# Rewriting the highway sum of a fused attention + highway kernel so that every VectorE step of it has an operand in PSUM

## The chip, the cores and the metric

One core of one Trainium2 chip. The metric is the device time of one execution in microseconds (us), medians over executions. An execution counts as slow when it lies more than 1.5% above the fastest of the same kernel; all runs told here are fast unless said. Engine names as in the profile: PE is TensorE, DVE VectorE, ACT ScalarE, POOL GpSimd, SP SyncE.

## The reference, cut to what matters

Cosine attention (8 batches, 12 heads, 448 positions, head size 64), then a highway layer over the 3584 x 768 result:

```python
def _moe_ref(x, w_h, w_t, b_t):
    H = np.maximum(x @ w_h, 0.0)
    T = 1.0 / (1.0 + np.exp(-(x @ w_t + b_t)))
    return (T * H + (1.0 - T) * x).astype(np.float32)
```

The kernel computes the sigmoid by tanh. With x standing for half of the reference's x, h for x @ w_h and t for tanh(x @ w_t + b_t/2), the result is (1+t) relu(h) - (t-1) x.

## The kernel before

The highway layer works in 28 tiles of 128 rows, each in two halves of 384 columns. Per half: 6 matmuls for the gate (plus one for the bias, or a bias add on DVE in the tail), 6 for h, tanh on ACT, and on DVE the gate g, the product and the output.

```python
def fg(ms=ms, mh=mh):                       # g = (t-1) x : two inputs in SBUF
    nc.vector.scalar_tensor_tensor(out=loc["g", mh][:, :], in0=loc["tt", mh][:, :],
        scalar=1.0, in1=xf()[:, ms], op0=ALU.subtract, op1=ALU.mult)
def fh(qi=qi, mh=mh):                       # h = (t+1) h : h in PSUM
    h = loc["pt", qi]
    nc.vector.scalar_tensor_tensor(out=h, in0=loc["tt", mh][:, :], scalar=1.0, in1=h, ...)
def fo(qi=qi, ms=ms, mh=mh):                # o = relu(h) - g
    nc.vector.scalar_tensor_tensor(out=loc["o"][:, ms], in0=loc["pt", qi], scalar=0.0,
        in1=loc["g", mh][:, :], op0=ALU.max, op1=ALU.subtract)
```

In the last six tiles (22 to 27; "the tail" below) both sums of a half lie in one two-bank PSUM tile, borrowed from the attention scores:

```python
if tail and w_i == 1 and grp[0] == 0:       # w_i == 1: the gate's matmuls, which come first
    loc["sp", mh] = s_ps.tile([128, 2, 512], FP32, name="sp")
...
loc["sp", mh][:, 1 - w_i, 0:MH] if tail else p_ps.tile([128, MH], FP32, name="pt", tag="pt")
```

The order of instructions on each engine comes from a list scheduler in the kernel (`Plan`), which models durations, buffers and the port that DVE and GpSimd share (`kind="lock"`). Semaphores are then set automatically, by tile. Strings such as `SQ_E` or `VM` assign each square, cast and copy to an engine.

## Time and profile before

| | kernel before |
|---|---|
| time, median | 292.5 us at the start, 291.5 to 291.9 in the later calls |
| granted PE clock in the profiled run | 0.98 |
| first output step of the highway layer | 59.1 us from the span's start |
| last output step before the tail (starts) | 246.6 us |
| last output step of all (starts) | 286.0 us |

The two positions in the middle of the table cut the run into a middle and a tail of 39.3 us; both kernels will be compared by them. One more view of the kernel before, ACT's timeline in the tail (start, duration, engine, line, operation, output and input, count; in brackets the idle time before it and what ended it):

```profile
265.83 0.49 ACT L847 ACTIVATE tt<-sp 128x384 f16<-128x384 f32 x1 [6.15 <-PE sp L818]
268.63 0.49 ACT L847 ACTIVATE tt<-sp 128x384 f16<-128x384 f32 x1 [2.32 <-PE sp L818]
```

Tanh reads the gate's sum, which was complete when the bias add ended, 0.8 us before each of the two tanhs; tanh was released by h's last three matmuls, which write the other bank of the same tile. That is how a wait by the whole tile looks: a releaser that computes nothing the waiter reads.

### The profile page before, as it was taken

Reading aid. Unit: us, or ns where it says so; the run is one execution under the profiler, and the core shown is the slowest. Engines: PE = TensorE matmul, PEld = TensorE weight load, DVE = VectorE, ACT = ScalarE, POOL = GpSimd, SP = SyncE. Lnnn points to the kernel's source line nnn. Section 1 sums busy time; section 2 is a strip of 40 time slices with the busy share of each in tenths; the row PEclk is TensorE's granted clock in tenths of the full one; section 3 lists DMA queues with packets and bytes.
Section 4 is the critical chain, followed back from the end, with each engine's and each line's share of the span. In section 5 each row is a group of like instructions: output and inputs, shape, how many; then the busy total and the mean of one; then the engine's idle time right before and its main releaser. Section 6 shows DMA issues by size and latency. Waiting matters only on the chain.

```text
span 290.9 us, 9872 instructions
## 1 busy us (share of the span) xinstructions
PE 244.1 (84%) x4229; PEld 137.8 (47%) x4229; DVE 238.2 (82%) x498; ACT 208.2 (72%) x284; POOL 138.6 (48%) x144
## 2 busy tenths in 40 slices
PE   0269777799888899999999999799999999887880
PEld 0226444454544455555545545356555555554440
DVE  3878918789999998999999989999975666696873
ACT  1398969979988899977987889668877767311120
POOL 3969558874468655962296836735900000000000
PEclk9999979989999999999999999999999999999996
DMA  7999929999999999999959999796757232112122
GB/s 259 375 353 292 257 52 309 212 284 326 247 273 243 287 179 369 289 182 284 356 123 248 164 287 283 146 235 132 157 119 147 85 85 56 56 56 81 56 108 54
DMA packets 72060, 58.94 MB, mean 203 GB/s; under 512 B 48336, under 2 KB 68304, under 8 KB 72016
## 3 DMA queue, kind: packets, MB, share of 16 engines
q1 hardware_dynamic: 70144, 55.49, 74.8%
q0 software_dynamic: 1600, 2.36, 4.5%
q8 instruction: 33, 0.54, 0.8%
q10 hardware_dynamic: 272, 0.46, 0.4%
q14 instruction: 11, 0.09, 0.1%
HBM read 38.14 MB, written 11.01 MB: 169 GB/s over the span
## 4 chain that ended last, share of the span: by engine, by line
PE 42%; DVE 25%; ACT 9%; DMA 7%; POOL 7%; issue 6%; SPq 2%; DVEq 0%; ACTq 0%; POOLq 0%
PE pt L818 17%; PE u L672 10%; PE sp L621 7%; ACT e L632 6%; DMA raw<-in_k_dram 6%; PE sp L818 5%; DVE g L851 3%; POOL qn L525 3%; DVE o L875 3%; DVE n L389 3%; DVE qn L525 3%; DVE x L723 2%; DVE pt L868 2%; DVE sp L837 2%; ACT tt L847 2%
## 5 line engine op out<-in xcount | busy, mean ns | idle before, releaser
L632 ACT ACTIVATE e<-sp 128x896 f16<-128x896 f32 x168 | 144.7, 920 | 21.3 <-PE sp L621 19.8
L818 PE MATMUL pt<-w,xT 128*128 128x384 f16 x528 | 102.3, 329 | 6.5 <-DVE o L875 3.4
L525 POOL TENSOR_TENSOR qn<-raw,rs 128x448 f16<-128x448 f32 x80 | 81.7, 1051 | 43.5 <-DVE rs L491 19.9
L818 PEld LDWEIGHTS <-xT 128*128 128x128 f16 x672 | 59.1, 98 | 62.5 <-issue 20.9
L621 PE MATMUL sp<-qT,qT 64*64 64x448 f16 x672 | 55.9, 379 | 8.3 <-ACT e L632 5.1
L672 PE MATMUL u<-vm,e 64*128 64x65 f16 x2688 | 58.3, 194 | 4.5 <-DVE x L723 3.4
L672 PEld LDWEIGHTS <-e 64*128 64x128 f16 x2688 | 48.7, 96 | 27.6 <-issue 17.2
L389 DVE TENSOR_REDUCE n<-sq 128x7 f32<-128x448 f16 x68 | 39.8, 609 | 2.9 <-ACT sq L365 2.4
L851 DVE SCALAR_TENSOR_TENSOR g<-tt,x 128x384 f16<-128x384 f16 x48 | 34.0, 708 | 9.3 <-ACT tt L847 9.2
L868 DVE SCALAR_TENSOR_TENSOR pt<-tt,pt 128x384 f32<-128x384 f16 x44 | 24.5, 557 | 9.1 <-PE pt L818 5.7
L847 ACT ACTIVATE tt<-pt 128x384 f16<-128x384 f32 x44 | 21.6, 492 | 14.2 <-ACT e L632 7.5
L621 PEld LDWEIGHTS <-qT 64*64 64x64 f16 x672 | 15.2, 106 | 33.5 <-issue 28.2
L818 PE MATMUL sp<-w,xT 128*128 128x384 f16 x144 | 25.4, 326 | 6.3 <-DVE o L875 2.9
L365 ACT ACTIVATE sq<-raw 128x896 f16<-128x896 f32 x29 | 26.9, 958 | 1.1 <-DMA raw<-in_k_dram 1.1
L847 ACT ACTIVATE tt<-sp 128x384 f16<-128x384 f32 x12 | 5.9, 490 | 29.9 <-DVE sp L837 16.9
L875 DVE SCALAR_TENSOR_TENSOR o<-pt,g 128x384 f32<-128x384 f32 x44 | 24.4, 554 | 1.3
L723 DVE TENSOR_TENSOR x<-u,rd 128x384 f16<-128x384 f32 x48 | 24.7, 552 | 0.7
L369 POOL TENSOR_TENSOR sq<-raw 128x448 f16<-128x448 f32 x17 | 17.7, 1038 | 15.0 <-DMA raw<-in_k_dram 6.1
L416 POOL TENSOR_TENSOR fold<-sq 128x448 f32<-128x448 f16 x14 | 15.0, 1085 | 13.4 <-ACT sq L365 13.4
L373 POOL TENSOR_TENSOR sq<-raw 128x448 f16<-128x448 f32 x17 | 17.8, 1049 | 0.0
L705 DVE RECIPROCAL rd<-u 128x12 f32<-128x12 f32 (+1 forms) x48 | 9.7, 202 | 9.9 <-PE u L672 9.4
L549 PE MATMUL tp<-ident,qn 128*128 128x128 f16 x63 | 6.7, 271 | 11.8 <-DVE qn L525 11.8
(46 smaller groups left out, 165.4 us busy)
## 6 DMA issues: line engine op xcount, KB each, us to landing
raw<-in_q_dram SPq DMA_DIRECT2D x24, 448.0 KB, 5.9
vr<-in_v_dram SPq DMA_DIRECT2D x24, 448.0 KB, 6.3
raw<-in_k_dram SPq DMA_DIRECT2D x23, 448.0 KB, 6.3
out_dram<-o SPq DMA_DIRECT2D x24, 384.0 KB, 3.9
out_dram<-o SPq DMA_DIRECT2D x8, 192.0 KB, 2.8
w<-in_moe_w_t_dram POOLq DMA_DIRECT2D x2, 576.0 KB, 10.2
w<-in_moe_w_h_dram POOLq DMA_DIRECT2D x2, 576.0 KB, 12.5
qT<-qn SPq DMA_TRANSPOSE x39, 4.5
```

The source lines that it names most:

```text
L365: nc.scalar.activation(o, i, AF.Square)
L389: nc.vector.reduce_sum(n2[:, qd, NT * t + g0 : NT * t + g0 + n], src()[:, g0 : g0 + n, 0:width], axis=AX.X,)
L525: (nc.vector if eng == "DVE" else nc.gpsimd).tensor_mul(st["qn", Q, t][:, :, :].rearrange("p c (h d) -> p h c d", h=2)[:, h0:h1, c0:c1, :] ...
L621: nc.tensor.matmul(sp[64 * half : 64 * half + 64, h, 0:S].rearrange("x (c p) -> x c p", c=C), lhsT=kT[hp, ci, 64 * half : 64 * half + 64], ...
L632: nc.scalar.activation(e[:, o : o + 2 * S].rearrange("x (a p c) -> x a p c", a=2, c=C), st["sp", Q, ci][:, :, 0:S].rearrange("x a (c p) -> ...
L672: nc.tensor.matmul(u[:, s, slot * (D + 1) : (slot + 1) * (D + 1)], lhsT=e[sp, o : o + 128], rhs=vm[sp, 2 * qd + h, c, 0 : D + 1], start=(c ...
L723: nc.vector.tensor_mul(st["x", b][:, :, 4 * qd : 4 * qd + 4, :].rearrange("p t (h s) d -> p t h s d", s=2)[:, :, :, s, :], u[:, s, :, 0:D] ...
L818: nc.tensor.matmul(loc["pt", qi], lhsT=loc["xT"][:, cc, :] if cc < CC else ones_row[:, :], rhs=w_f[w_i][:, cc, ms] if cc < CC else bth[:, ms],
L847: nc.scalar.activation(loc["tt", mh][:, :], loc["pt", qi], AF.Tanh)
L851: nc.vector.scalar_tensor_tensor(out=loc["g", mh][:, :], in0=loc["tt", mh][:, :], scalar=1.0, in1=xf()[:, ms], op0=ALU.subtract, op1=ALU.mult,
L868: nc.vector.scalar_tensor_tensor(out=h, in0=loc["tt", mh][:, :], scalar=1.0, in1=h, op0=ALU.add, op1=ALU.mult)
L875: nc.vector.scalar_tensor_tensor(out=loc["o"][:, ms], in0=loc["pt", qi], scalar=0.0, in1=loc["g", mh][:, :], op0=ALU.max, op1=ALU.subtract,)
```

## The change

The intent: write the result as x + x + (1+t)(relu(h)-x). The three DVE steps become relu(h)-x, times (1+t), plus 2x, and each has one operand in PSUM, so that none needs the port shared with GpSimd. In tiles 20 to 23 GpSimd computes (t-1)x instead, in two steps. ACT's switch to the tanh table becomes an operation that the plan knows. Assignment strings and one weight of the plan (LATE) are retuned.

```diff
-    LATE = 0.03
+    LATE = 0.025
...                                      (SQ_E, FOLDS, NORM, XT, VM retuned)
+    GATE = "RRRRRRRRRRRRRRRRRRRRPPPPRRRR"
+    BIAS = "MMMMMMMMMMMMMMMMMMMMMMDDDDDD"      (as before: DVE adds the bias in the tail)
-                carry = op("DVE", 470, None, [e] + waitg, fg, kind="lock")
+                    carry = op("DVE", 600, None, [e] + waitg, fg, kind="lock")      (GATE "D"; unused here)
+    SW_AT = 48
...
+                def fg1(...): nc.gpsimd.tensor_mul(g, tt, x)
+                def fg2(...): nc.gpsimd.tensor_sub(g, g, x)
+                if not switch:
+                    def fs(): nc.scalar.preload_act_table(AF.Tanh)
+                    switch.append(op("ACT", 1300, SW_AT, [("first", [z]) for z in logs], fs))
...
+            if not carry:                       # GATE "R"
+                def fd(...): h = max(h, 0) - x              # PSUM, SBUF -> PSUM
+                def fr(...): o = 2.0 * x + h                # SBUF, PSUM -> SBUF
+                e0 = op("DVE", 470, F + 3.2 + 3.2 * mh, [mms[-1]], fd)
+                e1 = op("DVE", 470, F + 3.5 + 3.2 * mh, [e0, e], fh)
+                e2 = op("DVE", 470, F + 4 + 3.2 * mh, [e1] + ..., fr)
```

(The bodies of fd, fr, fg1 and fg2 are shortened to what they compute.)

## The prediction

> **What bounds the kernel now.** I read the page first (busy shares, slices, groups), then busy time by stretch, then the chain of waits, and last the timeline of the end. No engine is full over the whole run:
>
> ```profile
> span 290.9 us, 9872 instructions
> ...
> PE 244.1 (84%) x4229; PEld 137.8 (47%) x4229; DVE 238.2 (82%) x498; ACT 208.2 (72%) x284; POOL 138.6 (48%) x144
> ```
>
> The stretches (columns: busy time and count of PE, PEld, DVE, ACT, POOL, then granted clock, DMA share, GB/s) show who is full when:
>
> ```profile
> 80.00:110.00 30.00, 26.71 (x499) 14.91 (x492) 28.99 (x63) 26.51 (x35) 20.00 (x22) 1.00 1.14 249
> 110.00:140.00 30.00, 29.71 (x532) 16.46 (x529) 28.33 (x60) 25.15 (x35) 18.52 (x19) 1.00 1.10 285
> ...
> 170.00:200.00 30.00, 26.71 (x482) 15.12 (x481) 28.89 (x62) 22.75 (x31) 14.05 (x13) 1.00 0.98 225
> 200.00:230.00 30.00, 29.82 (x555) 16.42 (x554) 22.82 (x47) 24.63 (x33) 11.16 (x12) 1.00 0.59 127
> ```
>
> DVE is at 94 to 97% from 80 to 200 us; PE is full at 110 to 140 and from 200 on. The chain of waits agrees: it lies mostly on PE from 98 to 142 and from 206 to 250, on GpSimd and on loads at about 148 to 174, almost wholly on DVE from 176 to 206, and after 250 alternates between PE, DVE and ACT. After 250 there are only the last six tiles of the highway layer (12 of the 56 half tiles).
>
> Because a busy PE is not PE at its peak, I counted its work. The chain gives 2.22 us for 13 FFN matmuls (0.171 each), 0.50 for 8 score matmuls (0.0625), 0.55 for 28 value matmuls (0.0196), 0.50 for 6 transposes. In 200 to 230 there were 97, 88, 364 and 6: 16.6 + 5.5 + 7.1 + 0.5 = 29.7 us, full, so the weights fit. The same sum gives need of 23.6 of 30 us in 50 to 80, 25.5 in 80 to 110, 29.5 in 110 to 140, 28.3 in 140 to 170 and 26.6 in 170 to 200. So between 50 and 200 PE has 6.4 + 4.5 + 0.5 + 1.7 + 3.4 = 16.5 us of slack that a faster DVE could let it close, but hardly any in 110 to 140 or from 200 to 250. In 250 to 291 the need is about 27 of 41 us.
>
> DVE's time holds a waste. Three kinds of instruction, all on 384 columns, make up a half tile:
>
> ```profile
> L851 DVE SCALAR_TENSOR_TENSOR g<-tt,x 128x384 f16<-128x384 f16 x48 | 34.0, 708 | 9.3 <-ACT tt L847 9.2
> L868 DVE SCALAR_TENSOR_TENSOR pt<-tt,pt 128x384 f32<-128x384 f16 x44 | 24.5, 557 | 9.1 <-PE pt L818 5.7 <-ACT tt L847 2.4 <-ACT sq L365 0.7
> L875 DVE SCALAR_TENSOR_TENSOR o<-pt,g 128x384 f32<-128x384 f32 x44 | 24.4, 554 | 1.3
> ```
>
> The two that have an operand in PSUM take 555 ns. The gate g, with both operands in SBUF, takes 708; singly it runs from 536 to 1354. Its busy time by stretch:
>
> ```profile
> 140.00:170.00 30.00, 6.48 (x7) 1.00 1.01 225
> 170.00:200.00 30.00, 5.16 (x7) 1.00 0.98 225
> ...
> 250.00:291.00 41.00, 6.69 (x12) 0.94 0.19 63
> ```
>
> After 230, where GpSimd has nothing to do, g takes 557 ns (6.69/12); at 140 to 170 it takes 926. That is what to see: g is long only beside a working GpSimd.
>
> **What the Trainium skill says.** "SBUF — State Buffer", section "Who interferes with whom": a DVE instruction with two SBUF inputs contends with a GpSimd instruction that reads SBUF, one with at most one SBUF input (outside the 2-port modes) doesn't, and the one that issues second blocks fully until the first ends. The trace agrees: 557 ns without GpSimd, up to 1354 with it, and 540 to 564 for the step with tt in SBUF and h in PSUM at any time. "VectorE: DVE Perf Modes", section "The TRN2 errata", gives (N+151)/0.96 ns for an fp32 tensor_tensor; for N=384 that is 557 ns, what the trace shows for these steps too, so swapping an SBUF operand for a PSUM one buys nothing but the lock. "GPSIMD Engine Reference", section "Elementwise", puts two-input work there at about half DVE's speed; the trace has 927 ns (shortest) for 448 columns. "ScalarE: Activation LUTs", section "What ACT_TABLE_LOAD costs", gives 1283 ns and a drain of some 1380; the trace shows 1283 at 54.95 but the tanh follows at 56.24, with no drain to see.
>
> **The change, part by part.**
>
> 1. *24 tiles (48 half tiles) replace g by relu(h)-x, and the output step takes 2x.* Still three DVE instructions per half tile, each with one PSUM operand, so 557 ns each. The waiting goes: 39.8 us for 56 g less 56 x 0.557 = 8.6 us. By stretch (g busy less count x 0.557): 1.2, 1.7, 1.3, 2.6, 1.3, 0.5 from 50 to 230, none after. About 6.8 us lies in stretches where PE has slack. GpSimd gains as well: its 80 normalizations average 1051 ns against a shortest of 927, its 34 squares 1040: about 13 us of waits, of which those against g go.
> The price: the new first step needs h, where g needed only tanh and could run during h's matmuls. After the h matmuls there are three DVE steps, not two, so a PSUM buffer stays taken some 0.5 us longer.
>
> 2. *Four tiles (20 to 23) put (t-1)x on GpSimd.* Eight half tiles lose one DVE step, 4.5 us, and gain two GpSimd steps of an estimated 0.8 to 0.9 us (927 ns scaled from 448 to 384). Tiles 20 and 21 fall in the PE-bound stretch, worth nothing on the path. Tiles 22 and 23 are the first of the last six, where DVE has 4.7 of 5 us in 255 to 260: 2.2 us of DVE less, but a gate 1.2 us slower, with a score buffer taken meanwhile. Net perhaps 0.5 us.
>
> 3. *Retuned assignments.* V casts on DVE: 16 half ones at 608 ns (9.7 us) and 6 whole at 973 (5.8) become 6 and 11. At the uncontended 0.62 us that is 10.5 us, at 973 it is 14.4: 1 to 5 us less; I take 2. xT copies on DVE 12 to 9: 1.7 us, all in the tail (tiles 23, 26, 27 go to DMA or ACT, which idles there). Normalizations on DVE 8 to 7: 1.4. The move of two of them away from 100 us and 189 us, both where DVE is full (1.07 and 1.83), against one new at about 200, is worth some 1.6 there. Squares move three from ACT to GpSimd (2.9 us off ACT, 6.3 us onto GpSimd, which is at 48%). Folds about even.
> DVE in all: 8.6 + 4.5 + 2 + 1.7 + 1.4, about 18 of 238 us.
>
> 4. *The table switch* as its own operation: at 54.95 it stands directly before the first tanh, PE's 7 matmuls follow that tanh in the chain, and the plan did not reckon with it. Moved to when the last Ln/Exp is done, it can save at most 1.3 us; as ACT is full there, 0.4.
>
> *The tail.* Per tile the last ones repeat every 5.35 us: 274.08 to 279.43. One buffer's cycle:
>
> ```profile
> 274.08 2.14 PE sp L818 x12
> 276.24 0.57 DVE sp L837
> 276.90 0.50 ACT tt L847
> 277.46 0.44 issue
> 277.90 0.33 DVE sp L868
> 278.36 0.56 DVE sp L837
> 278.92 0.47 DVE o L875
> 279.43 2.14 PE sp L818 x12
> ```
>
> The bias add, tanh, gate, product, the other half's bias add, output, then PE may refill. PE idles 1.28 us of it. If relu(h)-x ran beside tanh, 0.5 us per tile would go. But bias and tanh use one half of a score tile and h the other, and at 250 to 268 tanh is shown waiting for h's last three matmuls and h's matmuls for the bias add: waits go by the whole tile. So relu(h)-x will run before or after tanh, not beside it, and four steps stay in line. I count 0 to 0.5 us per tile for the last four tiles: 0.7 in all, and 0.9 for the copies taken off DVE.
>
> **Sum.** Middle: 6.8 (g) + 1.6 (normalizations) + 1 (casts in 80 to 200) = 9.4 us of DVE in stretches with 16 us of PE slack. Not all reaches the end: the chain there also passes over GpSimd, loads and PE, and the longer hold of PSUM takes some back. I credit a bit under half, 4.0. Switch 0.4, GpSimd gate 0.5, tail 1.6. Total 6.5: 292.5 - 6.5 = 286.0 us.
>
> **Rivals.**
> - *PE takes over.* The DVE time goes, but PE, full at 110 to 140 and 200 to 250, doesn't let it through: only the tail and part of 50 to 98 count, 2 to 4 us, about 289.5. For it: the PE chain at 98 to 142. Against: 16 us of PE slack elsewhere.
> - *Loads and GpSimd hold the middle.* From 148 to 174 the chain passes four GpSimd normalizations (3.97 us) and loads that take 5 to 7 us to land, with a DMA share near 1. With 6 us of squares and 15 us of gates more, GpSimd would give back part: about 288.5. Against: GpSimd idles half the time, and its waits fall.
> - *The longer PSUM hold* turns into PE waits for the output step (already 3.4 us for pt, 2.9 for sp); 48 half tiles at up to 0.5 us, a few per cent of which show: at worst 292.
> - *DVE was the bound throughout* and the 9 to 10 us come through nearly whole with 3 in the tail: 280 to 281.
>
> **Range and chances.** The sum's uncertain factor is the credited share. At a quarter, with nothing in the tail, 289.5; at nine tenths with the full tail, 281.5. The 2% line lies at 286.7, just above the centre, so faster is slightly likelier than same; slower needs the PSUM rival alone and, beyond 2%, a plan gone wrong.
>
> **What will show it.** Right: all three steps at 550 to 560 ns with hardly any over 600; DVE busy near 220 us; GpSimd's normalizations nearer 940; DVE below 94% in 140 to 200 and the chain moved onto PE there; one table load, away from the first tanh; the last tiles still 4.9 to 5.3 us apart. Wrong: the last tiles under 4.8 us apart (relu(h)-x beside tanh); steps still long beside GpSimd; PE waits for the output step up by 3 us or more; more than two table loads in all.

## The result, and the profile after

288.31 us (287.56 to 288.82, 4 executions) against 292.3 (290.71 to 295.23) beside it: ratio 0.988, interval 0.983 to 0.993. It is faster, by less than 2%. Ratios here and below are the mean time of one kernel's fast runs over that of the other's of the same rounds, so not quite the ratio of the medians quoted.

| | before | after | shift |
|---|---|---|---|
| first output step starts | 59.1 | 46.4 | -12.6 |
| last output step before the tail starts | 246.6 | 238.0 | -8.6 |
| last output step of all starts | 286.0 | 281.4 | -4.5 |
| tail (third less second row) | 39.3 | 43.4 | +4.1 |
| distance of the last tiles' ends | 5.35 | 6.47 | +1.12 |

So the middle gained twice what was forecast, and the tail gave back half of it.

From the page of the kernel after, the span and the engines' busy time, share and instructions:

```profile
span 286.2 us, 9911 instructions
...
PE 241.4 (84%) x4223; PEld 135.9 (47%) x4223; DVE 225.7 (79%) x481; ACT 206.5 (72%) x283; POOL 155.6 (54%) x166
```

DVE has 12.5 us less to do and GpSimd 17 more. The groups of the three steps (line, engine, operation, output and input, shapes, count; busy us, mean ns; idle before):

```profile
L893 DVE SCALAR_TENSOR_TENSOR pt<-tt,pt 128x384 f32<-128x384 f16 x44 | 24.7, 562 | 7.7 <-PE pt L821 4.6
...
L908 DVE SCALAR_TENSOR_TENSOR pt<-pt,x 128x384 f32<-128x384 f32 x36 | 20.2, 561 | 8.6 <-PE pt L821 8.3
...
L915 DVE SCALAR_TENSOR_TENSOR o<-x,pt 128x384 f32<-128x384 f16 x36 | 19.9, 552 | 1.0
```

No step is long any more: by line they run from 536 to 567 ns, where g had run to 1354. Instead of g's idle time before it (9.2 us, for tanh) the new first step has 8.3 us of waiting for h's matmuls. By stretch (PE, PEld, DVE, ACT, POOL, clock, DMA share, GB/s):

```profile
80.00:110.00 30.00, 28.21 (x513) 15.25 (x510) 27.52 (x65) 24.77 (x33) 21.61 (x23) 1.00 1.12 264
110.00:140.00 30.00, 28.32 (x520) 15.85 (x517) 27.05 (x59) 25.72 (x35) 19.90 (x20) 1.00 1.16 263
...
170.00:200.00 30.00, 28.58 (x523) 15.74 (x522) 28.34 (x62) 22.10 (x31) 17.76 (x18) 1.00 0.86 194
200.00:230.00 30.00, 29.84 (x554) 16.55 (x556) 17.39 (x38) 25.11 (x34) 6.29 (x7) 1.00 0.57 122
```

At 170 to 200 PE went from 26.7 to 28.6 us: its slack was used. (The kernel after is further on at the same time, so a stretch doesn't hold quite the same work; over 80 to 230 together PE went from 141.6 to 144.1 us.) DVE stays near 94% there; from 200 to 230 it has 17.4 us to do where the kernel before had 22.8.

The tail, in the chain of waits of the kernel after (start, duration, engine, output, line):

```profile
264.33 0.58 DVE sp L908
...
264.93 0.33 DVE sp L893
...
265.40 0.57 DVE sp L840
...
266.01 0.66 PE sp L821 x3
...
266.74 0.50 ACT tt L850
...
267.26 0.58 DVE sp L908
...
267.86 0.57 DVE sp L893
...
268.46 0.55 DVE o L915
269.01 0.49 DVE sp L840
...
269.54 0.66 PE sp L821 x3
...
270.27 0.50 ACT tt L850
...
270.80 0.58 DVE sp L908
```

From one relu(h)-x (L908) to the same step a tile later it is 6.47 us, and nothing in it runs beside anything else of the chain: the bias add (L840) lets h's last three matmuls go, they let tanh go, tanh lets relu(h)-x go. None of these three waits is for data that the waiter reads; the steps share a score tile. PE's timeline shows the stops, two per tile:

```profile
269.54 2.11 PE L821 MATMUL sp<-w,xT 128*128 128x384 f16 x12 [1.09 <-DVE sp L840]
272.48 2.17 PE L821 MATMUL sp<-w,xT 128*128 128x384 f16 x12 [0.83 <-DVE sp L840]
```

The kernel before had the same kind of wait, but its last three tiles ran all 24 matmuls in one go.

### The profile page after: what moved, and what is told of

It reads as the page before. It is cut to its first block, busy times and chain, and to the rows that moved or that the text cites. A ratio compares the mean times of both kernels' runs of the same rounds, so it can differ in the third digit from the quotient of the medians.

```text
span 286.2 us, 9911 instructions
## 1 busy us (share of the span) xinstructions
PE 241.4 (84%) x4223; PEld 135.9 (47%) x4223; DVE 225.7 (79%) x481; ACT 206.5 (72%) x283; POOL 155.6 (54%) x166
## 4 chain that ended last, share of the span: by engine, by line
PE 38%; DVE 31%; ACT 13%; POOL 7%; issue 5%; DMA 3%; ACTq 0%; DVEq 0%; POOLq 0%
PE pt L821 17%; ACT e L634 8%; PE u L674 8%; PE sp L623 7%; PE sp L821 5%; DVE o L915 4%; DVE n L391 4%; DVE pt L893 3%; DVE pt L908 3%; POOL qn L527 3%; DVE x L725 3%; ACT tt L850 2%; DVE sp L840 2%; DVE vm L586 2%; DVE qn L527 2%
## 5 line engine op out<-in xcount | busy, mean ns | idle before, releaser
L527 POOL TENSOR_TENSOR qn<-raw,rs 128x448 f16<-128x448 f32 x82 | 81.1, 1021 | 41.6 <-DVE rs L493 34.4
L674 PE MATMUL u<-vm,e 64*128 64x65 f16 x2688 | 57.6, 191 | 6.6 <-DVE x L725 4.5
L674 PEld LDWEIGHTS <-e 64*128 64x128 f16 x2688 | 47.3, 95 | 30.9 <-issue 18.2
L623 PE MATMUL sp<-qT,qT 64*64 64x448 f16 x672 | 55.3, 373 | 5.9 <-ACT e L634 4.5
L391 DVE TENSOR_REDUCE n<-sq 128x7 f32<-128x448 f16 x68 | 39.3, 610 | 1.1 <-ACT sq L367 0.3
L821 PE MATMUL sp<-w,xT 128*128 128x384 f16 x144 | 26.2, 325 | 10.0 <-DVE sp L840 8.9
L371 POOL TENSOR_TENSOR sq<-raw 128x448 f16<-128x448 f32 x20 | 20.1, 1007 | 16.4 <-DMA raw<-in_k_dram 7.9
L908 DVE SCALAR_TENSOR_TENSOR pt<-pt,x 128x384 f32<-128x384 f32 x36 | 20.2, 561 | 8.6 <-PE pt L821 8.3
L367 ACT ACTIVATE sq<-raw 128x896 f16<-128x896 f32 x26 | 24.4, 967 | 1.6 <-POOL fold L418 0.7
L915 DVE SCALAR_TENSOR_TENSOR o<-x,pt 128x384 f32<-128x384 f16 x36 | 19.9, 552 | 1.0
L375 POOL TENSOR_TENSOR sq<-raw 128x448 f16<-128x448 f32 x20 | 20.1, 1007 | 0.0
```

What stands on the lines that cost most here:

```text
L367: nc.scalar.activation(o, i, AF.Square)
L391: nc.vector.reduce_sum(n2[:, qd, NT * t + g0 : NT * t + g0 + n], src()[:, g0 : g0 + n, 0:width], axis=AX.X,)
L527: (nc.vector if eng == "DVE" else nc.gpsimd).tensor_mul(st["qn", Q, t][:, :, :].rearrange("p c (h d) -> p h c d", h=2)[:, h0:h1, c0:c1, :] ...
L623: nc.tensor.matmul(sp[64 * half : 64 * half + 64, h, 0:S].rearrange("x (c p) -> x c p", c=C), lhsT=kT[hp, ci, 64 * half : 64 * half + 64], ...
L674: nc.tensor.matmul(u[:, s, slot * (D + 1) : (slot + 1) * (D + 1)], lhsT=e[sp, o : o + 128], rhs=vm[sp, 2 * qd + h, c, 0 : D + 1], start=(c ...
L821: nc.tensor.matmul(loc["pt", qi], lhsT=loc["xT"][:, cc, :] if cc < CC else ones_row[:, :], rhs=w_f[w_i][:, cc, ms] if cc < CC else bth[:, ms],
```

## The experiments

Twelve kernels, three rounds each, in three calls; all gave the correct result. One matter goes ahead: most edits let the plan reorder everything. Three runs (tail_d, lock_back, split_fix) were made so that it could not: I compared the order of every engine's instructions with the changed kernel's, and it is the same, in tail_d up to the last four tiles. The same holds for before_split against the kernel before.

**after_again**: the changed kernel itself, as the yardstick.

> The changed kernel itself, as the yardstick on this chip. Both theories: 287.5 to 289 us, tail (from the first matmul of tile 22 to the last output step) about 43 us, first output step at about 46 us.

Measured 287.47 us (287.24 to 288.41), ratio 0.986. Tail 43.4 us, first output at 46.5 us, as before.

**lock_back**: is it the port?

```diff
 def fd(...):
     h = loc["pt", qi]
+    if n < 20: loc["g", mh] = ff_p.tile([128, MH], FP16, name="g")
+    d = loc["g", mh][:, :] if n < 20 else h
-    h = max(h, 0) - x
+    d = max(h, 0) - x
 def fh(...):
-    h = (tt + 1) * h
+    h = (tt + 1) * d            # two SBUF inputs in tiles 0 to 19
```

> Changed kernel, same order of every engine's instructions; in the first 20 tiles relu(h)-x goes to SBUF instead of PSUM, so that the product step has two SBUF inputs again (40 of the 48 half tiles). Theory A (the freed port is what made tile 22 start 9.2 us earlier): the product step grows from 562 to some 700 ns on average, 6 to 7 us of DVE, GpSimd's normalizations go from 1021 back to some 1050 ns, and the time grows by 4 to 7 us, to 292 to 295. Theory B (the lead comes from the first tiles starting 12.6 us earlier, and DVE had slack): the steps grow as much, but the time grows by 0 to 2 us, 288 to 290.

Measured 293.78 us (292.64 to 294.73), ratio 1.007: 6.3 us slower than the changed kernel by the medians, slower even than the kernel before. The product's group:

```profile
L894 DVE SCALAR_TENSOR_TENSOR pt<-tt,g 128x384 f32<-128x384 f16 x40 | 30.8, 770 | 3.8
```

770 instead of 562 ns in 40 half tiles is 8.3 us of DVE; by line they reach 1456 ns. GpSimd's normalizations went from 1021 to 1063 ns, and DVE's busy time as a whole rose by 7.0 us. The end of the middle moved from 238.4 to 244.6 us, +6.2, and the tail stayed at 43.4. Theory A holds, and this gives its exchange rate: of 8.3 us of waiting on DVE, 6.2 reach the end, three quarters. It is the rate for the product, which stands behind h's matmuls; the old g could run during them, and whether waiting in g costs as much isn't shown.

**tail_d**: the old gate in the last four tiles.

```diff
-    GATE = "RRRRRRRRRRRRRRRRRRRRPPPPRRRR"
+    GATE = "RRRRRRRRRRRRRRRRRRRRPPPPDDDD"
```

> Changed kernel with the old gate (t-1)x on DVE in the last four tiles only; the order is the same up to there. Theory T (in the tail relu(h)-x stands in line behind tanh and the matmuls, because waits go by the whole score tile): the last tiles go back from 6.47 to about 5.35 us apart, 3 to 4.5 us less in all, 284 to 285.5. Rival (the tail is longer because it starts with more work left, the same whichever gate): within 1 us of the changed kernel.

Measured 286.4 us (284.72 to 288.28), ratio 0.982: 1.1 us less by the medians. In the profiled execution the tail is 41.0 us, 2.4 less, and the last tiles end 5.3 to 5.6 us apart. (Its span, 282.9 us against 286.6, compares the fastest of four executions with the slowest of after_again's four, and 1.3 us of the difference lie in the middle, where the order is the same.) The mechanism shows in the trace, but the executions spread over 3.6 us and the median gains less than the theory asked. The new sum is dearer in the tail; it isn't the whole of it.

**split_fix**: the waits by whole tile. The gate's sums of the tail go to the one-bank tiles that the earlier tiles use; h keeps the score tile.

```diff
-                    if tail and w_i == 1 and grp[0] == 0:
+                    if tail and w_i == 0 and grp[0] == 0:
                         loc["sp", mh] = s_ps.tile([128, 2, 512], FP32, name="sp")
...
-                            loc["sp", mh][:, 1 - w_i, 0:MH] if tail
+                            loc["sp", mh][:, 0, 0:MH] if tail and w_i == 0
```

> Changed kernel, same order of every engine's instructions; in the last six tiles the gate's sums go to a PSUM buffer of their own (of the pair that the earlier tiles use) instead of the other half of h's score tile. Theory T (waits by the whole tile): h's matmuls no longer wait for the bias add, tanh no longer for h's last matmuls, relu(h)-x no longer for tanh; the last tiles come 4.6 to 5.2 us apart instead of 6.47 and the tail shrinks by 5 to 8 us, 280 to 283.5. Rival (DVE's eight steps a tile and their order set the 6.47 us): at most 1.5 us less.

Measured 277.21 us (276.78 to 277.37), ratio 0.950: 10.3 us less than the changed kernel, with no instruction moved. PE's timeline for one tile of the tail:

```profile
256.30 1.14 PE L821 MATMUL pt<-w,xT 128*128 128x384 f16 x6
257.27 1.14 PE L821 MATMUL sp<-w,xT 128*128 128x384 f16 x6
258.25 1.14 PE L821 MATMUL pt<-w,xT 128*128 128x384 f16 x6
259.23 1.14 PE L821 MATMUL sp<-w,xT 128*128 128x384 f16 x6
260.20 0.50 PE L773 MATMUL xp<-ident,xtail 128*128 128x128 f16 x6
260.78 1.14 PE L821 MATMUL pt<-w,xT 128*128 128x384 f16 x6
```

No idle time stands in brackets: PE goes on from half to half, and a tile takes 4.48 us instead of 6.47. The tail is 32.6 us instead of 43.4. The rival is out, and the gain exceeds even theory T's 5 to 8 us: the last tiles come closer than it asked, and tiles 22 and 23 gain as well (12.6 instead of 15.1 us). The split does two things at once, though: it takes away the waits between two halves of one tile, and each sum holds its buffer for a shorter time. This run doesn't tell the two apart.

**tail_order**: whole tiles kept, but h's matmuls not stopped by the bias add.

```diff
+            if w_i == 0 and "fb" in loc:
+                loc.pop("fb").deps.append(mms[-1])      # the plan puts the bias add after h's matmuls
```

> Changed kernel, whole score tiles kept, but in the last six tiles the plan places the bias add after all of h's matmuls, so that the matmuls don't stop for it. Theory T: PE's stops for the bias add (8.9 us) go, but bias add, tanh, relu(h)-x, product and output of a half still stand in one line; the last tiles come 5.0 to 5.8 us apart instead of 6.47: 284 to 286.5. If the stops of the matmuls were all of it, they come 4.5 us apart as with the split: 278 to 281.

Measured 285.81 us (284.89 to 286.76), ratio 0.980. PE's timeline:

```profile
265.32 2.12 PE L821 MATMUL sp<-w,xT 128*128 128x384 f16 x12 [0.72 <-DVE o L918]
268.16 2.12 PE L821 MATMUL sp<-w,xT 128*128 128x384 f16 x12 [0.72 <-DVE o L918]
```

PE now waits once per half, for the output step that frees the tile; 2.84 us per half, 5.68 per tile. With the other runs this makes a table of the last tiles' distance:

| | matmuls stopped by the bias add | not stopped |
|---|---|---|
| old gate | 5.6 (tail_d) | 5.35 (kernel before) |
| new sum | 6.47 (kernel after) | 5.68 (tail_order) |
| new sum, own PSUM tiles | | 4.3 to 4.5 (split_fix) |

(All but the kernel before have the x copies of the last three tiles on ACT; there they are on DVE or a DMA.) With the same copies, the stops cost 0.8 us per tile under the new sum (6.47 against 5.68), and the new sum 0.9 under the stops (6.47 against 5.6). Against the kernel before, whose copies differ, the new sum without stops costs 0.33 and the stops with the old gate 0.26; both together cost 1.12, much more than their sum. My reading, not tested, is that then no step of the chain is left that runs beside another. What the split brings beyond tail_order, another 1.2 to 1.4 us per tile, would be the rest of the one line and the shorter hold.

**before_split**: the edit of split_fix in the kernel before, same order of every engine as there.

> The kernel before, same order of every engine, with the same split of the tail's score tiles as in split_fix. If the whole-tile waits already cost the kernel before, its last tiles come 4.5 to 5 us apart instead of 5.35 to 6.2 and it gains 4 to 8 us: 284 to 288. If only the new sum suffers from them, it gains less than 1.5 us: 290 to 292.

Measured 287.23 us (286.64 to 289.36), ratio 0.9875; tail 34.9 instead of 39.3 us, last tiles 4.8 to 5.1 us apart. The waits by whole tile had cost the kernel before some 4 us already.

**old_tuning**: the changed kernel with SQ_E, FOLDS, NORM, XT, VM and LATE of the kernel before.

> Changed kernel (new sum, GpSimd gates, planned switch) with all retuned assignments and LATE put back to the kernel before. If the retuning brought the lead (first output step at 46 instead of 59 us), the first output goes back to 55 us or later and the time to 291 to 295; if the freed port brought it, the first output may be late but the lead grows along the middle and the time stays at 288 to 291.

Measured 288.09 us over all 12 executions; the 9 fast ones have a median of 287.41 us (285.01 to 289.08), ratio 0.986, the same as after_again. The first output came at 51.1 us, 4.5 later than with the new strings, but the end of the middle at 238.6 us, only 0.2 later than in after_again. The early start is worth nothing to be seen here: the lead of 4.5 us has gone by the end of the middle.

**tuning_only**: the new strings with the old gate and no planned switch.

```diff
-    GATE = "RRRRRRRRRRRRRRRRRRRRPPPPRRRR"
+    GATE = "DDDDDDDDDDDDDDDDDDDDDDDDDDDD"
...                                      (and the planned switch taken out, as in no_switch;
                                          the plan now takes g for 600 ns, in the kernel before for 470)
```

> The kernel before (old gate on DVE in all 28 tiles, no planned switch) with only the retuned assignments and LATE. Retuning theory: 287 to 290 us, first output at about 46. Port theory: 291 to 295, as the retuning was made for the other sum; g stays near 700 ns.

Measured 295.54 us (294.57 to 297.07), ratio 1.015: slower than the kernel before; g takes 706 ns in 48 of 56 half tiles. The new strings by themselves bring nothing. The slowdown isn't theirs alone for certain: the plan takes g to be longer here, and the granted clock was 0.964 to 0.977.

**no_switch**: the planned table switch taken out.

```diff
-                if not switch: ... switch.append(op("ACT", 1300, SW_AT, ...))
-                e = op("ACT", 390, None, [ready] + waitg + [("first", switch)], fa)
+                e = op("ACT", 390, None, [ready] + waitg + [("first", [z]) for z in logs], fa)
```

> Changed kernel without the planned switch; the table load stands again just before the first tanh, unplanned. The prediction gave the switch 0.4 us, at most 1.3: expected 287.5 to 289.5, table load at 44 to 47 us. If the planned switch is what moved the first tiles 11 us ahead, the load goes to 52 us or later and the time to 290 to 293.

Measured 289.42 us (286.95 to 290.91, 20 executions), ratio 0.993. In its trace the table load is at 45.8 us instead of 44.1, the first output step at 48.2 instead of 46.5, the end of the middle at 238.9 instead of 238.4, and the span 287.1 against 286.6. (That span of after_again is its slowest; the medians differ by 1.9 us.) The switch is not what moved the first tiles 11 us ahead; whether it is worth 0.5 or 1.9 us is left open.

**jitter**: nothing but the plan's slack factor from 1.30 to 1.32.

> Changed kernel with the plan's SLACK at 1.32 instead of 1.30 and nothing else: a measure of how much any edit that lets the plan reorder everything moves the time by itself. Expected within 2 us of the changed kernel, 286 to 290; a larger difference would take the meaning from the runs with another plan (the old assignments, no planned switch, other gates).

Measured 286.63 us (285.85 to 287.46), ratio 0.983: 0.8 us less than after_again, with the end of the middle 1.9 us earlier and the same tail of 43.4. It is one sample, but it shows that 1 to 2 us between kernels with different plans can't be taken for an effect of the edit.

**split_nop** and **split_p2r**: split_fix without GpSimd gates, and with them in tiles 20 and 21 only.

```diff
-    GATE = "RRRRRRRRRRRRRRRRRRRRPPPPRRRR"
+    GATE = "RRRRRRRRRRRRRRRRRRRRRRRRRRRR"      (split_nop)
+    GATE = "RRRRRRRRRRRRRRRRRRRRPPRRRRRR"      (split_p2r)
```

> split_fix without GpSimd gates: all 28 tiles use relu(h)-x on DVE. The four GpSimd tiles take 4.5 us off DVE at a time when DVE has 13 of 20 us and PE is the bound: expected 276 to 279 against 277.2. If the GpSimd gates carry weight: 280 or more.

> split_fix with GpSimd gates only in tiles 20 and 21. In tiles 22 and 23 the output step waited 2.1 us for GpSimd; with DVE's own form they should come 0.5 to 1 us faster: 276 to 277.5. If DVE is the bound there: 278 to 279.

split_nop: 279.98 us (278.97 to 280.41), 2.8 above split_fix, of which 1.5 lies in the middle and 1.3 in the tail; the expected upper end was passed, so the GpSimd gates may be worth a little, hardly separable from the plan's reordering. split_p2r: 275.76 us (275.63 to 276.57), ratio 0.946, the fastest of all, 5.4% below the kernel before and some 4% below the kernel after; tiles 22 and 23 take 12.2 instead of 12.6 us, a little less than the 0.5 to 1 us expected from GpSimd's wait there. That it beats split_fix by 1.4 us is within what a plan moves on its own.

## Why the prediction was right or wrong

The time (286.0 forecast, 288.3 measured) lies within the range and the change is faster, but below the 2% that was called slightly likelier. Two terms of the sum were mis-sized, in opposite directions, and that the total came near is their cancelling, which is luck. The total doesn't tell the theories apart either: two of the rivals stood at 288.5 and 289.5 us.

**What bounds the kernel**: right. DVE time taken away in the middle reached the end, and PE's slack there was what it used. One sign was wrongly named: DVE did not fall below 94% at 140 to 200 (28.93 and 28.34 of 30 us); more of the work lies in these stretches now (1120 of PE's matmuls against 1029).

**Three steps at 557 ns, 8.6 us of waiting gone**: right in duration (562, 561, 552). GpSimd's normalizations came to 1021, not to about 940. DVE's casts and normalizations stayed, and they too run long at times (whole casts 619 to 1358 ns, normalizations 1079 to 1814); that they hold GpSimd up is argued, not tested. DVE's busy time fell by 12.5 us, not 18. The groups' durations did fall by 18 (g's 39.8 us became 27.0, casts -1.3, normalizations -2.5, copies -1.5; 16.9 over all of DVE's instructions), but the recorded durations of neighbours overlap, so the engine gains less than their sum.

**"I credit a bit under half"**: the first term that failed. lock_back measured three quarters (6.2 of 8.3 us). The middle became 8.6 us shorter, where 4.4 were forecast with the switch. 6.2 of it is what lock_back took back through the port, with the order held. The rest, about 2.4, is not settled: it is neither the retuned strings (old_tuning) nor more than 1.9 us of the switch, and it is of the size by which a plan moves on its own (jitter).

**Still three DVE instructions, so the same cost**: a cost was missed. The pair g and product do not depend on each other and start 0.46 us apart at best (median 0.52 with the port's waits); relu(h)-x and product do, and start 0.66 us apart (median). In the middle no run takes it apart from the gain; in the tail it is probably part of the 0.33 us per tile.

**Retuned assignments (2.6 us of the DVE sum in the middle, 0.9 in the tail)**: not found. Without them the time is the same, and with them on the old gate (tuning_only, with its caveats) it is 4 us worse.

**Table switch, 0.4**: no run contradicts it, none settles it. The load moved from 54.95 to 43.97 us, and it was still directly before the first tanh, not away from it as I had said.

**GpSimd gates, 0.5**: the estimate of 0.8 to 0.9 us per step was good (912 ns), the gain was not there: tiles 22 and 23 took 15.1 us in both kernels.

**The tail, -1.6**: the second term that failed, and the larger. It was +4.1. The step is "I count 0 to 0.5 us per tile for the last four tiles". That waits go by the whole score tile and that four steps stay in line was read rightly from the trace. What I did not ask is what the plan does with it: it thinks relu(h)-x free to run beside tanh and the bias add free to run beside h's matmuls, and places both so that on the chip each waits for the last. PE stood 8.9 us for the bias add in the run's tail. I had read that stop in the kernel before at 250 to 268 us, where it hit two tiles, and took the 5.35 us of the last tiles as given.

**The rivals**: DVE as the bound throughout was nearest to the truth in the middle: with the tail unchanged, 8.6 us less would have been about 284. PE taking over is out there: it allowed 2 to 4 us. Loads and GpSimd holding the middle was not tested by a run; loads are 3% of the chain of waits after 7% before, GpSimd 7% in both. The longer hold of PSUM cost nothing to be seen in the middle: PE waited 1.2 us before its matmuls into pt, 6.5 in the kernel before.

The clock does not explain it: in the profiled runs both kernels were granted 1.00 from 66 us to the last output step, and so was lock_back in its tail. The kernel before had two early dips (0.79 at 36 to 44 us, 0.83 at 58 to 66) where the one after had none; what they cost was not tested, but old_tuning's loss of 4.5 us at that time was gone by the end of the middle.

## What to carry to other kernels

Before moving a step to where its operands allow more overlap, look which buffer it shares: if waits go by the whole tile, two results in one tile can become one chain, whatever the data say; giving one of them its own tile brought 10 us here without moving an instruction. Here, with DVE nearly full and GpSimd working beside it, an instruction with two SBUF inputs took 770 ns instead of 562, and three quarters of the difference reached the end. To test such a cost, hold the order of instructions fixed and move only an operand.

## What the Trainium skill lacked or had wrong

- "VectorE: DVE Perf Modes", section "The DRAIN you can't avoid", says that a semaphore after each operation cost nothing extra in a chain of copies. Here two neighbouring 384-column steps of which the second reads what the first wrote start 0.58 us apart at least (medians 0.59 to 0.66), independent ones mostly 0.46 to 0.48. The page gives no figure for a dependent pair.
- "PSUM — Partial Sum Buffer", section "PSUM bank collisions raise a hardware error", says that accesses of two engines to different banks run clean. In agreement, the split kernels were correct; but I found no page that says a tile of two banks may be guarded as one by the program's own semaphores, or what that costs: 43.4 us of tail against 32.6.
